# Layer 1 in another order: batch 0 is split around batch 1, and the weights are converted over 19 steps

## The chip, the cores and the metric

One core of a Trainium2 chip. The metric is the device time of one execution in microseconds (us), the median of several runs. TensorE is PE in the rows, VectorE DVE, ScalarE ACT, GpSimd POOL, SyncE SP.

## What is computed

Three stages in a row, over 4 batches of 512 tokens and 32 states, with 8 heads of 64:

```
scores = x @ state.T / 8        a  = softmax(scores)      xread = a  @ state
scores2 = state @ x.T / 8       a2 = softmax(scores2)     sread = a2 @ x
x1 = concat(xread, sread)                        # 2176 rows of 512
h  = x1 @ w_in  (512 x 2048);   g = h - tanh(h);          x2  = g @ w_out
h2 = x2 @ w_in2 (512 x 2048);   g2 = h2*tanh(softplus(h2)); out = g2 @ w_out2
```

The weights arrive as 64-bit floats, everything else as 32-bit floats.

## The kernel before

**Layer 1** runs in steps. A step is one column tile (128 of the 2048 inner columns) of one batch (512 tokens), so a batch has 16 steps, 0 to 15, and the state rows of all batches have 4 more. The list `seq` sets the order: batch 0, batch 1, batch 2, the states, batch 3.

In each step `up_x` makes the tile's 128x512 of h with six matmuls into one of two PSUM banks (h0, h1 in turn). It doesn't form x1: it multiplies the transposed softmax weights of the batch (`ath`, `atl`, a large and a small part) by the product of the states and w_in (`swp` when it is made, `swh` and `swl` when it is split), which `sw(b, c)` makes for four column tiles at a time. `elem1` then takes tanh on ScalarE (`t<-h`), subtracts on VectorE (`t<-h,t`), which frees the bank, and splits the result into `gh` (ScalarE) and `gl` (VectorE). Five steps later `down_x` multiplies this by w_out: 4 x 3 matmuls into four PSUM banks a0 to a3 (`acc`), which collect all 16 tiles of a batch and are then copied out to SBUF (`y`, or a half of a tile named `wide`), two by ScalarE and two by VectorE. For the first three tiles of batch 0 (`PLAIN`) nothing is split, and `down_x` issues 4 full-precision matmuls `acc<-t,w` in place of the 12.

**Weights.** A 128x512 piece of 64-bit weights is loaded by `load_next` into one of three `st` and three `wide` buffers; the queue `pending` sets the order of the loads. `conv_steps` makes it 32-bit: two ScalarE instructions (`w<-st` and `r<-st`, or `<-wide`), then one on VectorE (`w<-w,r`). Pieces i0 to i15 are of w_in, four for each group of four column tiles; pieces o0 to o15 are of w_out, one for each column tile, and are split too (`wh`, `wl`). Batch 0 uses each piece first; all the pieces then stay in SBUF for the later batches.

**Attention** of a batch is side work, hung on step numbers by `at(step, ...)`: transposes of x (`xtp`), scores (`sct`), their transposes (`sc`), maximum, subtraction, exp and norm (`mx`, `a`, `sm`), then `at_a`, which transposes the weights `a` (`atp`) and splits them into `ath`, `atl`. The other softmax goes through `at_exp_t`, `at_read_t` (`e2p`), `at_sread` (`srd`) and `at_sturn` (`srt`). Work on the second layer's weights (`bg`) runs beside layer 1, paced by the list `pace`; it stores its results through POOL's queue.

**Order.** Each engine works through its own queue in order. The first part of every queue, up to the bar in `FIRST_STEPS`, is pinned by hand; the rest is put in order by a scheduler when the kernel is built, by the order in which the code is written and by what has to be ready.

Layer 2 begins after layer 1's last step and takes nearly half of the time. The change does not touch its code.

Of the kernel before, what the change touches and what calls it, by code (L numbers as in the profile page):

```python
# [23 lines left out]
PLAIN = 3  # L24
# [2 lines left out]
MOST = 3  # L27
ROOM = 20
BACK = 2

# [8 lines left out]
FIRST_STEPS = """  # L39
    k4 s0 x0 X0 x1 X1 x2 X2 x3 X3 w0 w0 c0 C0 C1 k2 w0 t0 m0 t1 w1 w1 f0 b0 p0 P0 m1 e0 p1 P1 b1  # L40
    p2 e1 P2 u0 p3 P3 v0 y0 k6 w2 u1 v1 w2 h0 z2 q1 y1 h1 g0 l0 w1 l1 Q0 Q1 | f1 g1 w2 f2 g2
    w3 w3 w3 z2 f3 g3 w4 w4 w4
"""


class Unit:
# [29 lines left out]
def attention_moe_kernel(  # L76
# [296 lines left out]
    def conv_w1i(c, k):  # L373
        W1I[c, k] = conv32(("w1i", c, k))
# [6 lines left out]
    def conv_w1o(t):  # L381
        if t < PLAIN:
            W1O[(t,)] = conv32(("w1o", t))
        else:
            conv_split(W1O, ("w1o", t), t)

    def split_w1o(t):
        w = W1O[(t,)]
        W1O[(t,)] = split(w.t, name="w")
        put(w)  # L390

    def rows(w, t):
        return w[t * 128:(t + 1) * 128, :]
# [111 lines left out]
    def at_exp(b, j):  # L505
        sc_t(b, j)
        sc_max(b, j)
        sc_sub(b, j)
        sc_exp(b, j)
# [127 lines left out]
    def sw(b, c):  # L637
        if c:
            rhs = [[W1I[c, k].t for k in range(KD)]]
        else:  # L640
            rhs = [[w1i_tile(0, k, f) for k in range(KD)] for f in range(4)]
        ps = by_head("swp", b, rhs)
        for j in range(2):
            SW[b, c, j] = split(ps[j], name="sw")
        if b == B - 1:
            for k in range(KD):
                put(W1I.pop((c, k)))
            if not W1I:
                put(SB)
# [58 lines left out]
        return AC.activation(out=dst, in_=src, func=ACTF.Copy)  # L708

    def down_x(b, t):  # L710
        if t == 0:
            ACC[b] = [acc_bank(i) for i in range(KD)]
        if b == 0 and t < PLAIN:
            g = [G.pop((b, t))]
            w = W1O[(t,)]
        else:
            g = G.pop((b, t))
            wh, wl = W1O[(t,)]
        for i in range(KD) if b != 2 else (KD - 1, *range(KD - 1)):
            s = slice(i * 128, (i + 1) * 128)  # L720
            if len(g) == 1:
                TE.matmul(
                    out=ACC[b][i], lhsT=w.t[:, s], rhs=g[0].t, start=t == 0, stop=t == NT - 1
                )
            else:
                mm3p(
                    ACC[b][i], wh.t[:, s], wl.t[:, s], g[0].t, g[1].t, t == 0, t == NT - 1
                )
            if t == NT - 1:
                y = get("y")  # L730
                evac(y.t, ACC[b][i], i)
                Y[b, i] = y
        put(*g)
        if b == B - 1:
            put(*W1O.pop((t,)))
# [314 lines left out]
    wi = [  # L1050
        (("w1i", c, k), cols(w1i, c, k) if c else ftile(w1i, k)) for c in range(4) for k in range(KD)
    ]
    pending.extend(wi[:5])
    for t in range(NT):
        pending.append((("w1o", t), rows(w1o, t)))
        pending.extend(wi[5 + t:6 + t])
    for c in range(4):
        for k in range(KH):
            for j in (k, k + KH):
# [31 lines left out]
    seq = []  # L1091
    start = {}
    for b in (0, 1, 2, "s", 3):
        start[b] = len(seq)
        seq += [("x", b, t) for t in range(NT)] if b != "s" else [("s", c) for c in range(4)]
    start["2"] = len(seq)

    for s in range(16):
        at(s, lambda s=s: conv_w1o(s))
        if s < 11:  # L1100
            at(s, lambda s=s: conv_w1i((s + 5) // 4, (s + 5) % 4))
        if s in (2, 6, 11):
            at(s, lambda s=s: sw(0, s // 4 + 1))
        if s < PLAIN:
            at(start[1] + max(0, s - 1), lambda s=s: split_w1o(s))
    for b in (1, 2, 3):
        for c in range(4):
            at(start[b] + 4 * c - 2, lambda b=b, c=c: sw(b, c))
    for j in range(2):
        at(12 + j, lambda j=j: at_exp(1, j))  # L1110
        at(13 + j, lambda j=j: at_norm(1, j))
        for b in range(2):
            k = start[1] + 4 + 2 * b + 4 * j
            at(k, lambda b=b, j=j: at_exp_t(b, j), 1)
            at(k + 3 - b, lambda b=b, j=j: at_read_t(b, j), 1)
            if j:
                at(k + 4 - b, lambda b=b: at_sread(b), 1)
                at(k + 6 - b, lambda b=b: at_sturn(b), 1)
    when = {2: (3, 4, 5, 7, 8, 9, 10, 11, 12, 13, 15, 16), 3: (1, 3, 4, 5, 7, 8, 9, 11, 12, 12, 13, 15)}
    for b in (2, 3):  # L1120
        at(start[b - 1] - (b - 2), lambda b=b: load_x(b))
        for i, f in zip(when[b], at_steps(b), strict=True):
            at(start[b - 1] + i, f)
    for b in (1, 2, 3):
        at(start[b] - (3 if b > 1 else 1), lambda b=b: at_a(b))
    at(start[3], lambda: bg.extend(pieces_y(0) + list(late)))
    pace = [(start[1] + 8, 0), (start["s"], 52), (start["2"], 96)]
    done = [0]

    def keep_pace(i):  # L1130
# [101 lines left out]
        for t in tiles:  # L1232
            put(*(Unit(t[:, h * 512:(h + 1) * 512], None) for h in range(2)))

    at(start[1], widen)

    def up(q):
        if q[0] == "x":
# [89 lines left out]
```

## Time and profile before

| | us |
|---|---|
| median of 3 runs (714.16 to 715.76) | 715.24 |
| the profiled execution | 715.61 |
| its span, first to last instruction | 713.8 |
| TensorE busy in the span | 703.0 (98%) |
| VectorE busy | 467.0 (65%) |
| ScalarE busy | 350.7 (49%) |

The profiled execution is 1.8 us longer than its span, and 0.37 us longer than the median. Shares of busy time are means over very different stages. [...]

### The profile page before, as it was taken

The numbers are of one execution on the slowest core, as the hardware profiler recorded it, in microseconds if no ns is written. First come the engines' busy times: TensorE is split into PE (matmuls) and PEld (weight loads), VectorE is DVE, ScalarE is ACT, GpSimd is POOL, SyncE is SP. The second block draws the span as 40 slices with busy tenths as digits, with TensorE's granted clock in tenths as the row PEclk, the third lists the DMA queues.
The fourth block names the chain that finished last, engine by engine and source line by source line (L and its number), as shares of the span: only waits on it lengthen the run. The fifth ranks groups of instructions, "written<-read, shape, count | busy, mean of one in ns | idle before, by whom it ended". The sixth has DMA issues, their size and how long they took to land.

```text
span 713.8 us, 10569 instructions
## 1 busy us (share of the span) xinstructions
PE 703.0 (98%) x3978; PEld 562.3 (79%) x3978; DVE 467.0 (65%) x797; ACT 350.7 (49%) x631; POOL 70.5 (10%) x110
## 2 busy tenths in 40 slices
PE   8899999999999999999999999999999999999998
PEld 6467877777777898777878888888888888888886
DVE  5899855676659757898657875547753455545654
ACT  5999545555566656867546342234333223222320
POOL 0000010005202234410304100000000000000000
PEclk9999999999999999999999999999999999999999
DMA  9885110005536458692958654444966244322003
GB/s 289 318 309 189 61 59 2 31 30 171 217 109 213 163 184 274 203 356 91 344 213 299 225 174 153 145 141 134 313 208 199 93 159 157 124 77 85 1 1 132
DMA packets 52643, 118.66 MB, mean 166 GB/s; under 512 B 7280, under 2 KB 11632, under 8 KB 52592
## 3 DMA queue, kind: packets, MB, share of 16 engines
q1 hardware_dynamic: 44272, 90.72, 38.1%
q0 software_dynamic: 8320, 27.27, 10.5%
q8 instruction: 31, 0.51, 0.3%
q14 instruction: 20, 0.16, 0.1%
HBM read 88.34 MB, written 29.62 MB: 165 GB/s over the span
## 4 chain that ended last, share of the span: by engine, by line
PE 87%; ACT 5%; issue 2%; DMA 2%; DVE 2%; POOL 1%; SPq 1%; POOLq 0%; ACTq 0%
PE acc L63 48%; PE h L63 32%; PE swp L63 2%; PE hs L63 2%; ACT r L63 1%; ACT w L63 1%; DMA x<-in_x_dram 1%; DMA wide<-in_x_dram 1%; PE xtp L63 1%; POOL wi L261 1%; ACT t L63 1%; DVE wide L63 1%; ACT gh L63 1%; PE sct L63 1%; PE e2p L63 0%
## 5 line engine op out<-in xcount | busy, mean ns | idle before, releaser
L63 PE MATMUL acc<-wo,gh 128*128 128x512 f32 (+1 forms) x548 | 168.1, 388 | 0.0
L63 PE MATMUL h<-yh,ws 128*128 128x512 f32 x448 | 156.8, 391 | 0.1
L63 PEld LDWEIGHTS acc<-wo,gh 128*128 128x128 f32 x548 | 102.1, 188 | 20.9 <-ACT gh L63 0.4
L63 DVE TENSOR_TENSOR wide<-acc,wide 128x512 f32<-128x512 f32 (+1 forms) x92 | 62.9, 684 | 74.6 <-PE acc L63 73.3
L63 PE MATMUL acc<-wo,gl 128*128 128x512 f32 (+1 forms) x274 | 106.3, 388 | 0.0
L63 PE MATMUL acc<-gh,wh 128*128 128x512 f32 x244 | 99.4, 408 | 0.0
L63 PEld LDWEIGHTS h<-yh,ws 128*128 128x128 f32 x448 | 84.1, 188 | 17.8 <-DVE mt L63 0.5
L63 PE MATMUL acc<-gh,wl 128*128 128x512 f32 x244 | 95.7, 392 | 0.0
L63 PE MATMUL acc<-gl,wh 128*128 128x512 f32 x244 | 95.2, 390 | 0.0
L63 PE MATMUL h<-yl,ws 128*128 128x512 f32 x224 | 87.3, 390 | 0.0
L63 DVE TENSOR_TENSOR wide<-h,wide 128x512 f32<-128x512 f32 x94 | 64.6, 687 | 27.9 <-ACT wide L63 13.9
L63 DVE TENSOR_TENSOR gl<-wide,gh 128x512 fp32r<-128x512 f32 x72 | 49.7, 690 | 47.4 <-ACT gh L63 47.3
L63 ACT ACTIVATE wide<-wide 128x512 f32<-128x512 f32 x47 | 29.7, 632 | 85.3 <-DVE wide L63 85.3
L63 ACT ACTIVATE wide<-h 128x512 f32<-128x512 f32 x41 | 24.4, 596 | 81.0 <-PE h L63 80.1
L63 PEld LDWEIGHTS acc<-wo,gl 128*128 128x128 f32 x274 | 51.4, 188 | 11.0 <-DVE gl L63 0.4
L63 PEld LDWEIGHTS acc<-gh,wh 128*128 128x128 f32 x244 | 45.9, 188 | 17.5 <-issue 5.6
L63 PEld LDWEIGHTS acc<-gh,wl 128*128 128x128 f32 x244 | 45.8, 188 | 11.4 <-issue 1.2
L63 PE MATMUL h<-ath,swh 128*128 128x512 f32 x128 | 51.5, 403 | 1.8 <-DVE t L63 1.0
L63 PEld LDWEIGHTS acc<-gl,wh 128*128 128x128 f32 x244 | 46.0, 188 | 8.4
L63 PE MATMUL h<-ath,swl 128*128 128x512 f32 x128 | 50.4, 394 | 0.0
L63 PE MATMUL h<-atl,swh 128*128 128x512 f32 x128 | 50.0, 390 | 0.0
L63 ACT ACTIVATE gh<-wide 128x512 fp32r<-128x512 f32 x72 | 45.5, 631 | 7.3 <-DVE wide L63 5.5
(168 smaller groups left out, 1019.9 us busy)
## 6 DMA issues: line engine op xcount, KB each, us to landing
ws<-wi SPq DMA_DIRECT2D x128, 256.0 KB, 3.9
wo<-wo SPq DMA_DIRECT2D x64, 256.0 KB, 3.9
st<-in_moe_w_in_dram SPq DMA_DIRECT2D x27, 512.0 KB, 5.7
st<-in_moe_w_out_dram SPq DMA_DIRECT2D x22, 512.0 KB, 4.9
wi<-wh POOLq DMA_DIRECT2D x32, 256.0 KB, 3.8
wi<-wl POOLq DMA_DIRECT2D x32, 256.0 KB, 4.4
wide<-in_moe_w_out_dram SPq DMA_DIRECT2D x10, 512.0 KB, 5.3
wo<-wh POOLq DMA_DIRECT2D x16, 256.0 KB, 5.6
```

Of the source, the lines that this page charges most:

```text
L63: i = fn(*args, **kw)
L261: nc.gpsimd.dma_start(out=d, in_=v if len(d.shape) == 2 else v.rearrange("p (g e) -> p g e", g=2))
```

## The change

`seq` now takes the first four tiles of batch 0, all 16 of batch 1, the other 12 of batch 0, then batch 2, the states and batch 3 as before. The sums of batch 0's first four tiles leave the four PSUM banks after tile 3 (two copies on ScalarE and two on VectorE) and wait in SBUF; when the other 12 tiles are done, four VectorE additions put the two parts together, where four copies stood before. So the four banks are handed over at one place more than before: after batch 0's tile 3, after batch 1, after batch 0's tile 15, after batch 2.

Layer 1 starts with pieces i0 to i3; i4 is no longer converted ahead of the first step. The list `CONVERTED` gives the pieces of each of 19 steps, and the loads come in that order; before, the steps 0 to 15 took one piece of w_out each and the first eleven a piece of w_in too. What batch 1 needs for its first step (exp and norm of both halves, `at_a`) moves from steps 12 to 15 to steps 0 to 3. The products of the states and w_in come two steps ahead of use as before, by batch and group. The other softmax of batches 0 and 1 moves from steps 20 to 31 to steps 12 to 21, that of batch 2 stays, and for batch 3 the first transposes of x go from steps 33 and 35 to step 35. The background work starts at step 22 in place of 24.

```diff
-    w3 w3 w3 z2 f3 g3 w4 w4 w4
+    w3 w3 w3 z2 f3 g3
...
+CONVERTED = (
+    "o0", "o1 i4", "o2", "o3 i5", "i6", "o4 i7", "i8 o5", "i9 o6", "i10 i11", "o7 i12", "o8 i13",
+    "o9 i14", "o10 i15", "o11", "o12", "o13", "o14", "o15",
+)
...
     def down_x(b, t):
-        if t == 0:
+        starts = t in ((0, PART) if b == 0 else (0,))
+        stops = t in ((PART - 1, NT - 1) if b == 0 else (NT - 1,))
+        if starts:
             ACC[b] = [acc_bank(i) for i in range(KD)]
...
-            if t == NT - 1:
+            if stops and (b, i) in Y:
+                V.tensor_tensor(out=Y[b, i].t, in0=ACC[b][i], in1=Y[b, i].t, op=ALU.add)
+            elif stops:
                 y = get("y")
                 evac(y.t, ACC[b][i], i)
...
-    for b in (0, 1, 2, "s", 3):
-        start[b] = len(seq)
-        seq += [("x", b, t) for t in range(NT)] if b != "s" else [("s", c) for c in range(4)]
+    for b, ts in (
+        (0, range(PART)), (1, range(NT)), (0, range(PART, NT)), (2, range(NT)), ("s", range(4)),
+        (3, range(NT)),
+    ):
+        start.setdefault(b, len(seq))
+        seq += [("x", b, t) if b != "s" else (b, t) for t in ts]
...
-    for s in range(16):
-        at(s, lambda s=s: conv_w1o(s))
-        if s < 11:
-            at(s, lambda s=s: conv_w1i((s + 5) // 4, (s + 5) % 4))
-        if s in (2, 6, 11):
-            at(s, lambda s=s: sw(0, s // 4 + 1))
-        if s < PLAIN:
-            at(start[1] + max(0, s - 1), lambda s=s: split_w1o(s))
...
+    for t in range(PLAIN):
+        at(PART + t, lambda t=t: split_w1o(t))
...
-        at(12 + j, lambda j=j: at_exp(1, j))
-        at(13 + j, lambda j=j: at_norm(1, j))
...
+        at(j, lambda j=j: at_exp(1, j))
+        at(1 + j, lambda j=j: at_norm(1, j))
+    for b, times in ((0, (12, 13, 13, 15, 16, 17)), (1, (15, 16, 16, 17, 20, 21))):
...
-    when = {2: (3, 4, 5, 7, 8, 9, 10, 11, 12, 13, 15, 16), 3: (1, 3, 4, 5, 7, 8, 9, 11, 12, 12, 13, 15)}
+    when = {2: (3, 4, 5, 7, 8, 9, 10, 11, 12, 13, 15, 16), 3: (3, 3, 4, 5, 7, 8, 9, 11, 12, 12, 13, 15)}
...
-    pace = [(start[1] + 8, 0), (start["s"], 52), (start["2"], 96)]
+    pace = [(start[2] - 10, 0), (start["s"], 52), (start["2"], 96)]
```

**What this moves on the engines.** First place: TensorE between its fourth tile of h (batch 0, tile 3) and its fifth. Before, the full-precision sums stand among the tiles, and the product for batch 0's tiles 4 to 7 (`swp`, eight wide matmuls) comes ahead of tile 4:

```order
L63 MATMUL acc_554<-t,w 128x512
L63 MATMUL acc_555<-t,w 128x512
L63 MATMUL acc_552<-t,w 128x512
L63 MATMUL swp<-w,sbt 32x512 x8
L63 MATMUL acc_553<-t,w 128x512
L63 MATMUL h<-ath,swh 128x512
L63 MATMUL h<-atl,swh 128x512
L63 MATMUL acc_554<-t,w 128x512
```

Now the fifth tile is batch 1's first. The product for batch 1 (32 narrow matmuls) and both transposes of batch 1's softmax weights stand ahead of it:

```order
L70 MATMUL acc_605<-t,w 128x512
L70 MATMUL acc_606<-t,w 128x512
L70 MATMUL acc_607<-t,w 128x512
L70 MATMUL acc_608<-t,w 128x512
L70 MATMUL swp<-w,sbt 32x128 x32
L70 MATMUL acc_605<-t,w 128x512
L70 MATMUL acc_606<-t,w 128x512
L70 MATMUL acc_607<-t,w 128x512
L70 MATMUL atp<-ident,a 128x128 x4
L70 MATMUL acc_608<-t,w 128x512
L70 MATMUL atp<-ident,a 128x128 x4
L70 MATMUL h<-ath,swh 128x512 x2
```

Eight of the twelve full-precision matmuls have moved behind tile 3, and two transposes of `a`, which stood behind tile 15, now stand ahead of tile 4. The second transpose has one such matmul between it and the first.

Second place: VectorE around its seventh and eighth subtraction `t<-h,t`. Before, between these two:

```order
L63 TENSOR_TENSOR t<-h,t 128x512
L63 SCALAR_TENSOR_TENSOR w<-w,r 128x512
L63 CAST wh<-w 128x512
L63 TENSOR_TENSOR gl<-t,gh 128x512
L63 TENSOR_TENSOR swl<-swp,swh 128x512 x2
L63 TENSOR_TENSOR wl<-w,wh 128x512
L63 SCALAR_TENSOR_TENSOR w<-w,r 128x512 x3
L63 TENSOR_TENSOR t<-h,t 128x512
```

Now, between the same two:

```order
L70 TENSOR_TENSOR t<-h,t 128x512
L70 CAST wh<-w 128x512
L70 TENSOR_TENSOR wl<-w,wh 128x512
L70 TENSOR_TENSOR gl<-t,gh 128x512
L70 TENSOR_TENSOR wl<-w,wh 128x512
L70 TENSOR_TENSOR swl<-swp,swh 128x512 x2
L70 COPY y<-acc_606 128x512
L70 COPY y<-acc_608 128x512
L70 TENSOR_TENSOR t<-h,t 128x512
```

The copies of the second and fourth bank are new; they stand behind a `gl` and two `swl`, which wait for ScalarE's `gh` and `swh`. ScalarE's copies of the first and third bank stand right behind that `gh`, with one `r<-st` between them.

Third place: TensorE at the first turn of a state read (`srt`, batch 0's). Such side products share two PSUM banks with `swp`, in turn. Before, the turn stands in the middle of a step's sums, shortly behind the products for batch 2, whose banks VectorE's `swl` frees:

```order
L63 MATMUL swp<-w,sbt 32x128 x32
L63 MATMUL acc_1307<-gh,wh 128x512
L63 MATMUL acc_1307<-gl,wh 128x512
L63 MATMUL acc_1307<-gh,wl 128x512
L63 MATMUL acc_1308<-gh,wh 128x512
L63 MATMUL acc_1308<-gl,wh 128x512
L63 MATMUL acc_1308<-gh,wl 128x512
L63 MATMUL acc_1309<-gh,wh 128x512
L63 MATMUL acc_1309<-gl,wh 128x512
L63 MATMUL acc_1309<-gh,wl 128x512
L63 MATMUL srt<-ident,wide 128x128
L63 MATMUL acc_1310<-gh,wh 128x512
```

Now batch 0's turn comes in step 17, behind a whole tile of h:

```order
L70 MATMUL h<-atl,swh 128x512
L70 MATMUL h<-ath,swl 128x512
L70 MATMUL h<-ath,swh 128x512
L70 MATMUL h<-atl,swh 128x512
L70 MATMUL h<-ath,swl 128x512
L70 MATMUL srt<-ident,sr 128x128
L70 MATMUL e2p<-ident,scs 128x128 x4
L70 MATMUL acc_797<-gh,wh 128x512
```

The nearest products of a group stand three tiles of h ahead of it; before, nine sums lay between.

## Rows read from the trace of the kernel before

**Rows 1.** The page: busy time, and TensorE in 40 slices of the span.

```profile
PE 703.0 (98%) x3978; PEld 562.3 (79%) x3978; DVE 467.0 (65%) x797; ACT 350.7 (49%) x631; POOL 70.5 (10%) x110
...
PE   8899999999999999999999999999999999999998
```

**Rows 2.** Waits of TensorE: waited for, us in total, times, longest.

```profile
PE h L63 <- DVE t L63: 1.0, 1, 1.0
...
PE xtp L63 <- DMA wide<-in_x_dram: 0.9, 1, 0.9
PE h L63 <- ACT swh L63: 0.7, 1, 0.7
PE srt L63 <- DVE swl L63: 0.6, 1, 0.6
PE swp L63 <- DVE w L63: 0.6, 2, 0.3
```

**Rows 3.** Windows: length, busy PE, PEld, DVE, ACT, POOL, then clock, DMA share, GB/s.

```profile
20.00:40.00 20.00, 17.93 (x126) 9.48 (x125) 17.24 (x34) 20.00 (x44) 0.00 (x0) 1.00 0.86 313
40.00:60.00 20.00, 19.74 (x90) 13.86 (x89) 18.57 (x32) 19.95 (x38) 0.00 (x0) 1.00 0.85 301
160.00:180.00 20.00, 19.26 (x207) 14.79 (x207) 12.74 (x25) 12.24 (x23) 10.14 (x14) 1.00 0.52 175
180.00:200.00 20.00, 19.12 (x102) 14.65 (x100) 11.56 (x20) 11.07 (x20) 4.92 (x7) 1.00 0.48 181
```

**Rows 4.** Timeline of TensorE: start, us, what, [idle before, releaser].

```profile
23.79 0.45 PE L63 MATMUL swp<-w,sbt 64*32 64x128 f32 x16
25.28 0.47 PE L63 MATMUL h<-ath,swh 128*128 128x512 f32 x1 [1.03 <-DVE t L63]
...
41.58 3.60 PE L63 MATMUL acc<-t,w 128*128 128x512 f32 x8
44.61 0.79 PE L63 MATMUL h<-ath,swh 128*128 128x512 f32 x1
...
54.58 0.39 PE L63 MATMUL acc<-gh,wl 128*128 128x512 f32 x1
54.80 0.39 PE L63 MATMUL h<-ath,swh 128*128 128x512 f32 x1
...
73.75 0.60 PE L63 MATMUL sc<-ident,scs 128*128 128x128 f32 x4
74.11 0.48 PE L63 MATMUL acc<-gh,wh 128*128 128x512 f32 x1
...
82.95 1.16 PE L63 MATMUL swp<-w,sbt 64*32 64x128 f32 x64
```

**Rows 5.** Timeline of ScalarE, same columns.

```profile
21.38 0.71 ACT L63 ACTIVATE r<-wide 128x512 uint32<-128x512 uint32 x1
...
23.05 0.63 ACT L63 ACTIVATE t<-h 128x512 f32<-128x512 f32 x1
...
28.00 0.74 ACT L63 ACTIVATE w<-st 128x512 f32<-128x512 f32 x1
28.55 0.74 ACT L63 ACTIVATE r<-st 128x512 uint32<-128x512 uint32 x1
29.11 0.67 ACT L63 ACTIVATE t<-h 128x512 f32<-128x512 f32 x1
29.59 0.75 ACT L63 ACTIVATE w<-wide 128x512 f32<-128x512 f32 x1
```

**Rows 6.** Timeline of VectorE: two instructions back to back, and two copies of banks.

```profile
48.13 0.68 DVE L63 TENSOR_TENSOR t<-h,t 128x512 f32<-128x512 f32 x1
48.73 0.68 DVE L63 SCALAR_TENSOR_TENSOR w<-w,r 128x512 uint32<-128x512 uint32 x1
...
105.12 1.28 DVE L63 COPY wide<-acc 128x512 f32<-128x512 f32 x2
```

**Rows 7.** Chain that ended last, the load of batch 3's x.

```profile
176.39 6.49 DMA wide<-in_x_dram
```

More of the change, by code (lines that the diff above doesn't have):

```diff
@@ L29 @@
 BACK = 2
+PART = 4
 FIRST_LOADS = "s0123wwt4567wwww"
@@ L722, in down_x @@
                 TE.matmul(
-                    out=ACC[b][i], lhsT=w.t[:, s], rhs=g[0].t, start=t == 0, stop=t == NT - 1
+                    out=ACC[b][i], lhsT=w.t[:, s], rhs=g[0].t, start=starts, stop=stops
                 )
@@ L726, in down_x @@
                 mm3p(
-                    ACC[b][i], wh.t[:, s], wl.t[:, s], g[0].t, g[1].t, t == 0, t == NT - 1
+                    ACC[b][i], wh.t[:, s], wl.t[:, s], g[0].t, g[1].t, starts, stops
                 )
-            if t == NT - 1:
+            if stops and (b, i) in Y:
+                V.tensor_tensor(out=Y[b, i].t, in0=ACC[b][i], in1=Y[b, i].t, op=ALU.add)
+            elif stops:
                 y = get("y")
@@ L1052, in attention_moe_kernel @@
     ]
[L1053 to L1056, printed above, removed]
+    pending.extend(wi[:KD])
+    for key in " ".join(CONVERTED).split():
+        n = int(key[1:])
+        pending.append((("w1o", n), rows(w1o, n)) if key[0] == "o" else wi[n])
     for c in range(4):
@@ L1106, in attention_moe_kernel @@
-    for b in (1, 2, 3):
-        for c in range(4):
-            at(start[b] + 4 * c - 2, lambda b=b, c=c: sw(b, c))
-    for j in range(2):
-        at(12 + j, lambda j=j: at_exp(1, j))
-        at(13 + j, lambda j=j: at_norm(1, j))
[L1112 to L1118, printed above, removed]
@@ L1119, in attention_moe_kernel @@
-    when = {2: (3, 4, 5, 7, 8, 9, 10, 11, 12, 13, 15, 16), 3: (1, 3, 4, 5, 7, 8, 9, 11, 12, 12, 13, 15)}
+    for b, ts in (
[4 more added lines that the diff above has]
+        seq += [("x", b, t) if b != "s" else (b, t) for t in ts]
+    start["2"] = len(seq)
+    for s, keys in enumerate(CONVERTED):
+        for key in keys.split():
+            n = int(key[1:])
+            if key[0] == "o":
+                at(s, lambda n=n: conv_w1o(n))
+            else:
+                at(s, lambda n=n: conv_w1i(n // KD, n % KD))
@@ new lines, in attention_moe_kernel @@
+    for t in range(PLAIN):
+        at(PART + t, lambda t=t: split_w1o(t))
+    for b in range(B):
+        for c in range(not b, 4):
+            k = seq.index(("x", b, 4 * c)) - 2
+            at(k, lambda b=b, c=c: sw(b, c))
+    for j in range(2):
+        at(j, lambda j=j: at_exp(1, j))
+        at(1 + j, lambda j=j: at_norm(1, j))
+    for b, times in ((0, (12, 13, 13, 15, 16, 17)), (1, (15, 16, 16, 17, 20, 21))):
+        for k, f in zip(
+            times,
+            (
+                lambda b=b: at_exp_t(b, 0), lambda b=b: at_read_t(b, 0),
+                lambda b=b: at_exp_t(b, 1), lambda b=b: at_read_t(b, 1),
+                lambda b=b: at_sread(b), lambda b=b: at_sturn(b),
+            ),
+            strict=True,
+        ):
+            at(k, f, 1)
@@ L1120, in attention_moe_kernel @@
+    when = {2: (3, 4, 5, 7, 8, 9, 10, 11, 12, 13, 15, 16), 3: (3, 3, 4, 5, 7, 8, 9, 11, 12, 12, 13, 15)}
     for b in (2, 3):
-        at(start[b - 1] - (b - 2), lambda b=b: load_x(b))
+        at(16 * (b - 1) - 2 * b + 5, lambda b=b: load_x(b))
         for i, f in zip(when[b], at_steps(b), strict=True):
-            at(start[b - 1] + i, f)
+            at(16 * (b - 1) + i, f)
     for b in (1, 2, 3):
@@ L1233, in widen @@
             put(*(Unit(t[:, h * 512:(h + 1) * 512], None) for h in range(2)))
-    at(start[1], widen)
+    at(len(CONVERTED), widen)
     def up(q):
```

## Prediction

> **What bounds the kernel now.** The page first: TensorE is busy for 703.0 of 713.8 us, and in the 40 slices it falls below 9 tenths only in the first two and the last [rows 1]. So there are 10.8 us of idle TensorE at most, and a change that issues the same matmuls, as this one does, can win only a part of them. The view of TensorE's waits says where they lie [rows 2]: leaving out the start (first loads, first transposes), a tile of h waits 1.0 us for a subtraction on VectorE and another 0.7 us for `swh`, the products of the groups 0.6 us for converted weights, a turn of the state read (`srt`) 0.6 us and a transpose of batch 3's x 0.9 us for its load. The windows put the first three into 20 to 60 us, where ScalarE is busy 20.00 and 19.95 of 20 us, and the last two into 160 to 200 us, where TensorE lacks 0.74 and 0.88 us [rows 3]. [...]
>
> ScalarE's 40 full microseconds are conversions. One half of a conversion follows the other after 0.55 to 0.56 us, and a tanh takes 0.48 us until the next begins [rows 5]. VectorE starts one per 0.60 us [rows 6]. The clock of this stretch is thus ScalarE's queue, and TensorE waits where it needs something that stands deep in it. That makes the sum below a matter of queue positions: what stands ahead of the thing waited for.
>
> **The change part by part.**
>
> *The first tile's subtraction.* Two halves of i4 no longer stand ahead of the first tanh: ScalarE goes from the `r` at 21.38 straight to it, at 21.9 in place of 23.05 [rows 5]. The subtraction then ends near 23.7, before the small products end at 24.24 (23.79 and 0.45), and the third tile starts there and not at 25.28: the 1.03 us wait goes [rows 4]. The 0.7 and 0.6 us in rows 2 hang on batch 0's tile 4 and on early pieces of w_in; tile 4 is no longer the fifth tile, so these go as well. That is 2.3 us off.
>
> *What comes in their place.* Batch 1's first tile is the fifth one now. Its transposes (`atp`) take the two banks of the products right before them, so they wait for VectorE's two `swl`; the second waits for the last norm multiplication too, which stands behind these two, a reciprocal and a `gl`. Those wait for ScalarE's `swh` and `gh`. Ahead of that `gh`, from the `r` at 21.38 on, the changed kernel's order gives ScalarE 16 conversion halves, 4 tanh, 5 full instructions of other kinds (taken as 0.52, between the two) and 4 small ones (no row shows one alone; taken as 0.33): 9.0 + 1.9 + 2.6 + 1.3 = 14.8, so `gh` starts at 36.2. VectorE gets through `swl`, reciprocal, `gl` and the multiplication at about 38.2. TensorE arrives earlier. From 24.24 it has two tiles of h (six matmuls of 0.22 each, 1.35), both `sc` (0.36 and a slow start behind it, 0.4 each: 73.75 to 74.11), eight full-precision matmuls, the products (1.1: 82.95 and 1.16 less the overlap) and one `atp`, taken as an `sc` of the same shape. Four full-precision ones take 3.03 us and stretch the next by 0.40 (41.58 to 44.61, 0.79 in place of 0.39), so 0.86 each [rows 4]. That is 24.24 + 2.7 + 0.8 + 6.9 + 1.1 + 0.4 = 36.1: a new wait of about 2 us.
>
> *The hand-over after batch 0's tile 3.* Batch 1's first sums need the banks. Up to the `gh` of the seventh tile ScalarE has 30 halves, 7 tanh, 15 others and 6 small ones from 21.38 on: 16.8 + 3.4 + 7.8 + 2.0 = 30.0, so it starts at 51.4 and ends at 52.0 (0.6 us). Behind it VectorE has `gl`, `wl`, two `swl` (four at 0.60) and then the copy of the second bank; two copies of a bank took 1.28, so 0.64 [rows 6]: free at 55.0. Then three banks' sums, nine matmuls, 2.0: the fifth tile's sums, which follow the eighth tile of h, end at 57.0. Before, the sums at this place ended at 54.80 [rows 4]. The new order has two `sc` and two `atp` more in front of this point, 1.7 to 1.8 us that are saved later, so 56.6 would be even. TensorE itself would be at the second bank at 54.80 - 2.0 + 1.8 - 2.3 + 2.0 = 54.3, earlier than 55.0, so the copy ends last. **The early stretch gives nothing: 0.4 us worse**, with ScalarE's queue setting the time as before. The bounds: 2.3 us better (no new wait) and 1.5 us worse, if VectorE idles ahead of the copy as it did in 40 to 60 us, 1.4 of 20 us [rows 3], so 1.1 us in the 15 us between the two places.
>
> Past this point ScalarE has less to do per step than before and catches up; loads are not late either, since each piece is converted later than the piece of the same number in the queue of loads was before, and ScalarE did not idle for one in 20 to 60 us [rows 3].
>
> *The late waits.* Batch 3's x is loaded in step 31 still, and its first transpose comes two steps later, about 9 us; the load took 6.49 us from issue [rows 7], and the wait was 0.9. It goes. The turn that waited 0.6 for `swl` no longer follows the products that hold its bank: three tiles of h lie between. It goes too. By the windows both are worth **1.6 us** [rows 3]. The bounds are 1.6 and 0 (other reads and turns, moved to steps 12 to 21, wait as long).
>
> *The other hand-overs.* After batch 0's tile 15 VectorE makes four additions from PSUM. The trace has none of this form from this stage in the rows; a copy of a bank took 0.64, so 2.6 for four if they begin when the last sum ends. A tile of h and two transposes of x cover 2.2. Between 0 and 0.4, taken as 0.1, since the first three banks are done ahead of the last. Before, the same four banks changed hands after batch 0, with copies at 105.12 [rows 6], and the waits show nothing for it [rows 2]. [...]
>
> **Sum.** +0.4 - 1.6 + 0.1 = -1.1 us on the profiled span of 713.8. The profiled execution (715.61, 1.8 us around the span) is 0.37 above the median, so I put the difference to the median: 715.24 - 1.1 = **714.1 us**. A difference of 0.2%, 1.43 us, is about what a measurement of this kernel can tell from no change; this one is smaller.
>
> **The rivals.**
>
> *No new wait at the hand-over.* If VectorE gets through its queue sooner than the 0.60 steps say, ScalarE's own copies are last: the first starts at 51.9, the second behind one `r` at 53.0, free at 53.6, and two banks' sums end at 55.0, 1.6 better than 56.6. With the late waits gone: 715.24 - 1.6 - 1.6 = 712.0. For it: TensorE's distance to the copy is only 0.7 us. Against it: VectorE was busy 18.57 of 20 us there [rows 3]. 0.18.
>
> *The late waits stay, elsewhere.* The reads of batches 0 and 1 now stand in steps 12 to 21, behind conversions that run until step 18. 715.24 + 0.4 + 0.1 = 715.7. 0.18.
>
> *Slower: background work.* It starts two steps earlier, while batch 0 still has ten tiles and batch 2's attention is under way. Before, the 40 us in which POOL first stores its results are the ones in which TensorE waits 1.62 us [rows 3], 0.04 per us: a turn or transpose waits for what a conversion delays on VectorE or in POOL's queue. At this rate over the 80 us of steps 14 to 31 it is 3.2 in place of 1.6, so 715.24 + 0.5 + 1.6 = 717.3. It decides from 2.5 us of waits in that stretch on. Against it: VectorE is busy for 12 of 20 us there. 0.12.
>
> *The hand-overs are not covered.* TensorE stands for all four additions, 2.6 in place of 0.1: 716.6. The hand-over of before speaks against it [rows 2, 6]. 0.05. [...]
>
> **How the numbers follow.** My forecast has 0.47, and about half of it, with the early stretch 0.3 better than worked out, is over the 1.43 us. Faster: 0.18 + 0.24 = 0.42. Same: 0.23 + 0.18 + 0.02 = 0.43. Slower: 0.12 + 0.03 = 0.15. The range goes from below the first rival, 711.6 (the early bound would give 711.4), to 716.5, which leaves out most of the third and half of the fourth; the forecast's own is 713.0 to 715.4.
>
> **What would show it.** The third tile of h starts at 24.2 with no wait on VectorE; a wait of about 2 us on VectorE's `a` at the second `atp`, at 36 to 38 us; a wait of 0.5 to 1.5 us at the second bank of the first batch 1 sums, on the copy of `y`, and their end near 57; ScalarE full from 20 to 55 us and with gaps from 62 us on; no TensorE wait for batch 3's x, none at a `srt`. The forecast fails if the two early waits are missing (then ScalarE is not the clock that I take it for), or if the windows of 100 to 200 us lack more than 1.6 us of TensorE.

## The result and the profile after

The changed kernel takes 719.16 us (median of 4 runs, 718.32 to 720.61), the kernel before 714.91 on the same chip (714.16 to 715.76). The ratio is 1.0058, with a 95% interval of 1.0042 to 1.0073: 0.6% slower, clear of no change, and outside the range that was predicted. The profiled execution of the changed kernel took 719.03 us with a span of 717.3, against 713.8 before.

The page (busy time; then PE, its load of weights left out, and the granted clock in 40 slices) answers to [rows 1]:

```profile
PE 704.4 (98%) x3978; PEld 564.2 (79%) x3978; DVE 467.8 (65%) x801; ACT 351.4 (49%) x631; POOL 70.5 (10%) x110
...
PE   8999999999899998999999999999999999999998
```

Idle TensorE has grown from 10.8 to 12.9 us, and PE's own busy time from 703.0 to 704.4. The matmuls are the same, and the granted clock of the whole was 0.997 (1.000 in the kernel before), so a part of this is a slower clock, whose place is found below. The slices fall below 9 tenths in the first, the eleventh (179 to 197 us), the fourteenth (233 to 251), the sixteenth (269 to 287) and the last; the three in the middle are new, and in the fourteenth the timeline shows no idle time. TensorE's waits (us in total, times, longest), against [rows 2]:

```profile
PE acc L70 <- DVE y L70: 2.4, 2, 1.4
PE acc L70 <- DVE wide L70: 2.1, 1, 2.1
PE warm L70 <- DVE warm L1200: 1.5, 1, 1.5
PE sc L70 <- DVE swl L70: 1.3, 1, 1.3
PE atp L70 <- DVE swl L70: 0.6, 1, 0.6
PE xtp L70 <- DVE swl L70: 0.6, 1, 0.6
PE atp L70 <- ACT r L70: 0.5, 1, 0.5
```

All five waits of before are gone, and six other lines have come (the seventh, `warm`, is at the start of both kernels). The windows say where (columns as in [rows 3]):

```profile
20.00:40.00 20.00, 18.93 (x157) 10.75 (x157) 18.79 (x40) 20.00 (x43) 0.00 (x0) 1.00 0.88 287
40.00:60.00 20.00, 18.96 (x102) 13.44 (x101) 18.86 (x33) 19.52 (x38) 0.00 (x0) 1.00 0.76 253
...
100.00:180.00 80.00, 79.93 (x607) 62.16 (x606) 49.61 (x93) 43.13 (x78) 15.72 (x22) 1.00 0.31 99
180.00:200.00 20.00, 18.05 (x95) 13.62 (x95) 13.42 (x22) 12.87 (x23) 4.36 (x8) 1.00 0.70 234
200.00:240.00 40.00, 38.72 (x228) 29.38 (x227) 30.26 (x63) 24.22 (x46) 9.49 (x14) 1.00 0.40 132
240.00:280.00 40.00, 37.93 (x354) 33.45 (x353) 26.99 (x48) 26.30 (x47) 14.42 (x22) 1.00 0.73 251
280.00:320.00 40.00, 40.00 (x194) 31.05 (x193) 33.49 (x54) 26.25 (x48) 7.99 (x13) 0.96 0.41 145
```

Up to 180 us the changed kernel is no worse than the old one; 100 to 180 us is full. What it loses lies in three places from 180 us on, and behind the third the clock is down (0.96 in the last window, with no idle time). TensorE's timeline there, and at the early places that the prediction named:

```profile
18.12 0.47 PE L70 MATMUL h<-ath,swh 128*128 128x512 f32 x1
...
23.10 0.50 PE L70 MATMUL h<-ath,swh 128*128 128x512 f32 x1
...
34.89 0.66 PE L70 MATMUL atp<-ident,a 128*128 128x128 f32 x4 [0.59 <-DVE swl L70]
...
36.88 0.63 PE L70 MATMUL atp<-ident,a 128*128 128x128 f32 x4 [0.47 <-ACT r L70]
...
53.50 0.50 PE L70 MATMUL acc<-gh,wh 128*128 128x512 f32 x1 [1.04 <-DVE y L70]
...
55.68 0.39 PE L70 MATMUL h<-ath,swh 128*128 128x512 f32 x1
...
188.82 0.66 PE L70 MATMUL xtp<-ident,wide 128*128 128x128 f32 x4 [0.56 <-DVE swl L70]
...
191.30 0.47 PE L70 MATMUL acc<-gh,wh 128*128 128x512 f32 x1 [1.39 <-DVE y L70]
...
230.70 0.66 PE L70 MATMUL sc<-ident,wide 128*128 128x128 f32 x4 [1.28 <-DVE swl L70]
...
279.51 0.56 PE L70 MATMUL acc<-wh,gh 128*128 128x512 f32 x1 [2.07 <-DVE wide L70]
279.87 0.63 PE L70 MATMUL acc<-wl,gh 128*128 128x512 f32 x1
280.30 0.63 PE L70 MATMUL acc<-wh,gl 128*128 128x512 f32 x1
```

At 191.30 the additions after batch 0's tile 15 look guilty. VectorE's timeline shows that they begin late:

```profile
186.70 0.68 DVE L70 TENSOR_TENSOR swl<-swp,swh 128x512 fp32r<-128x512 f32 x1
187.48 0.69 DVE L70 TENSOR_TENSOR gl<-wide,gh 128x512 fp32r<-128x512 f32 x1
188.09 0.68 DVE L70 TENSOR_TENSOR swl<-swp,swh 128x512 fp32r<-128x512 f32 x1
188.69 2.47 DVE L70 TENSOR_TENSOR y<-acc,y 128x512 f32<-128x512 f32 x4
```

The products (`swp`) were done at 183.9, the sums of tile 15 at 186.9. `swl` waits for `swh`, and `swh` stands in ScalarE's order behind a conversion. ScalarE's timeline, at this place and at the states' hand-over:

```profile
176.20 0.63 ACT L70 ACTIVATE gh<-wide 128x512 fp32r<-128x512 f32 x1 [0.20 <-DVE wide L70]
180.81 0.66 ACT L70 ACTIVATE r<-st 128x512 uint32<-128x512 uint32 x1 [3.98 <-DMA wi<-wl]
181.37 0.66 ACT L70 ACTIVATE wide<-st 128x512 f32<-128x512 f32 x1
182.83 0.63 ACT L70 ACTIVATE wh<-wide 128x512 fp32r<-128x512 f32 x1 [0.80 <-DVE wide L70]
183.37 0.58 ACT L70 ACTIVATE wide<-h 128x512 f32<-128x512 f32 x1
...
185.84 0.59 ACT L70 ACTIVATE swh<-swp 128x512 fp32r<-128x512 f32 x1
...
187.35 0.58 ACT L70 ACTIVATE swh<-swp 128x512 fp32r<-128x512 f32 x1
...
225.50 0.63 ACT L70 ACTIVATE wh<-w 128x512 fp32r<-128x512 f32 x1 [2.70 <-DMA wi<-wl]
...
274.55 0.68 ACT L70 ACTIVATE w<-st 128x512 f32<-128x512 f32 x1 [2.12 <-DMA st<-in_moe_w_out_dram]
...
276.75 1.05 ACT L70 ACTIVATE swh<-swp 128x512 fp32r<-128x512 f32 x2
```

This is the reading that matters. For 3.98 us ScalarE stands, that is, does nothing: the next instruction in its order is the `r` of a background piece, and the slot (a 128x512 buffer in SBUF) that it writes to is still being stored by POOL (`wi<-wl`). The tanh of the tile of h that TensorE had finished at 178.9 waits behind it until 183.37, then the two `swh`, VectorE's `swl`, the additions, the banks. Nothing overtook the `r` in these 3.98 us. Nor does anything elsewhere: in the trace of the changed kernel all 801 of VectorE's instructions begin in the order of the program, and ScalarE's do too.

At 225.50 the same happens for another store (2.70 us), ahead of the wait at 230.70; at 274.55 for a load that hasn't landed (2.12 us), ahead of `gh`, `swh`, `swl` and the copies of batch 2's banks.

The length of a stand alone doesn't say what it costs. The kernel before has one of 3.25 us, and the changed kernel with the start at step 24 (experiment 4) one of 4.27, and TensorE has no wait in the ten microseconds behind either:

```profile
246.39 0.66 ACT L63 ACTIVATE w<-st 128x512 f32<-128x512 f32 x1 [3.25 <-DMA wi<-wl]
```

```profile
262.36 0.66 ACT L70 ACTIVATE w<-st 128x512 f32<-128x512 f32 x1 [4.27 <-DMA st<-in_moe_w_in_dram]
```

The three that the changed kernel pays for end 3 to 8 us ahead of TensorE's wait, with the `swh` of new products and, at two of them, banks that change hands in between.

### The profile page after: what moved, and what is told of

The parts are those of the page before. It is cut to its first block, busy times and chain, and to the rows that moved or that the text cites. A ratio compares the mean times of both kernels' runs of the same rounds, so it can differ in the third digit from the quotient of the medians.

```text
span 717.3 us, 10593 instructions
## 1 busy us (share of the span) xinstructions
PE 704.4 (98%) x3978; PEld 564.2 (79%) x3978; DVE 467.8 (65%) x801; ACT 351.4 (49%) x631; POOL 70.5 (10%) x110
## 4 chain that ended last, share of the span: by engine, by line
PE 70%; issue 15%; ACT 6%; POOL 5%; DVE 3%; DMA 1%; POOLq 0%; ACTq 0%; DVEq 0%
PE acc L70 39%; PE h L70 26%; POOL wi L268 3%; PE hs L70 2%; ACT w L70 1%; ACT r L70 1%; POOL wo L268 1%; PE swp L70 1%; DMA wi<-wh 1%; ACT wh L70 1%; ACT gh L70 1%; PE xtp L70 1%; ACT t L70 0%; DVE wl L70 0%; ACT swh L70 0%
## 5 line engine op out<-in xcount | busy, mean ns | idle before, releaser
L70 DVE TENSOR_TENSOR wide<-acc,wide 128x512 f32<-128x512 f32 (+1 forms) x78 | 53.3, 683 | 61.8 <-PE acc L70 60.5
L70 DVE TENSOR_TENSOR wide<-h,wide 128x512 f32<-128x512 f32 x103 | 70.8, 687 | 27.9 <-ACT wide L70 15.8
L70 DVE TENSOR_TENSOR gl<-wide,gh 128x512 fp32r<-128x512 f32 x81 | 55.9, 691 | 48.2 <-ACT gh L70 47.9
L70 ACT ACTIVATE wide<-h 128x512 f32<-128x512 f32 x51 | 30.3, 594 | 83.8 <-PE h L70 82.4
L70 ACT ACTIVATE gh<-wide 128x512 fp32r<-128x512 f32 x81 | 51.2, 632 | 13.7 <-DVE wide L70 11.9
```

What stands on the lines that cost most here:

```text
L70: i = fn(*args, **kw)
```

## The experiments

Theory A: the background pieces, two steps earlier, make ScalarE stand for stores and loads, and TensorE's new waits come from there. Theory B: the hand-over with its four additions costs by itself. All are edits of the changed kernel. Nothing of the computation is left out in any run.

**1. Pieces held to the counts of the kernel before** (`ran_before` is the list of them by step).

```
-                goal = n0 + (n1 - n0) * (i + 1 - s0) / (s1 - s0)
+                goal = ran_before[i]
```

> The changed kernel with one thing put back: the number of background pieces that have run after each step follows the list of the kernel before (1 piece by step 24, 8 by step 31, 40 by step 48), not the changed kernel's own pace (6, 13 and 46). Theory A, background work: pieces that run earlier make ScalarE stand for a store (4.0 us ahead of 180.8) and for a load (2.1 us ahead of 274.6), and TensorE's waits of 2.0 us at 188 to 191, 1.3 at 230 and 2.1 at 278 us with the slower clock behind it (1.6) come from there. Then these waits go and the time is 719.2 - 5 to 7 = 712 to 714.5 us. Theory B, the hand-over: the four additions on VectorE after batch 0's tile 15 are the price wherever the pieces stand. Then the wait of 1.4 us at the first sums behind it stays, and those at 230 and 278 us, which follow other work, stay as well: 718 to 720 us.

713.73 us, ratio 0.9992 (0.9978 to 1.0006). The waits at 188 to 191 and at 278 are gone, with the additions in place; one of 1.29 us at 229 stays. Theory A. The list was only a ceiling: for want of free slots 7 pieces had run by step 32, where the kernel before had run 11.

**2. Copies at the hand-over, additions later.**

```
-                V.tensor_tensor(out=Y[b, i].t, in0=ACC[b][i], in1=Y[b, i].t, op=ALU.add)
+                z = get("z")
+                evac(z.t, ACC[b][i], i)
+                at(37 + i, lambda i=i, z=z: add_y(b, i, z))
```

> The changed kernel with its background pace kept, but the four banks of batch 0's second part are copied out as batch 0's were in the kernel before (two copies on ScalarE, two on VectorE, into four more slots), and the four additions follow in SBUF three to six steps later. Theory A (background work): VectorE is late for another reason, ScalarE's stand ahead of it, so of the 2.0 us at 188 to 191 at least 1 stays, and the other waits as well: 717.5 to 719.5 us. Theory B (the hand-over): the wait of 1.4 us on VectorE's y goes: 717.5 us or less, with no stand at this place. The slots taken may move pieces by a few steps; the windows around 180 to 200 us are what is read.

718.56 us, 1.0051 (1.0036 to 1.0066). TensorE still waits at the same place, 2.69 us for `swl` and 0.79 for a copy, behind a stand of ScalarE of 3.40 us for a store. Theory B falls. (`add_y`, not shown, adds the copy to the first part in SBUF.) The waits at 230 and 278 are gone, which theory A did not foresee: up to step 35 the pieces run as in the changed kernel, but from step 36 on the four slots taken put them up to eight pieces behind it.

**3. Both.**

> Both edits at once: background pieces held to the counts of the kernel before, and the four additions later in SBUF behind copies. If the two losses are of different origin they add up and this is the fastest of the four: 711.5 to 713.5 us. Theory A alone gives the same as the pieces alone within 0.7 us; theory B alone the same as the copies alone.

722.42 us, 1.0121 (1.0086 to 1.0156): a miss by 9 us. Between steps 36 and 52 the four slots more push the pieces back two to six behind experiment 1, and ScalarE stands for loads, 3.80 us ahead of 276.5 the longest; TensorE waits 2.1 us at 250, 2.88 at 280 and 1.22 at 324. So neither the additions nor the mean lead of the pieces decides, but what stands where.

**4. Only the start of the pace, 24 in place of 22.**

```
-    pace = [(start[2] - 10, 0), (start["s"], 52), (start["2"], 96)]
+    pace = [(start[2] - 8, 0), (start["s"], 52), (start["2"], 96)]
```

> The changed kernel with only the start of the background pace put back, from step 22 to step 24; the rest of the pace and the additions stay. Theory A with the start as its cause (my rival of the prediction: two steps earlier): most of the loss at 180 to 240 us goes, 714 to 717 us. If the cause is not the start but which slot a piece takes and which store or load is still under way at that moment, the pieces catch up within some steps and new stands appear at other places: 716 to 720 us. Theory B: 719 us, as the changed kernel.

713.61 us, 0.9983 (0.9973 to 0.9992): 5.5 us come back from one number. VectorE and TensorE at the hand-over of batch 0, additions unchanged:

```profile
186.86 0.68 DVE L70 TENSOR_TENSOR swl<-swp,swh 128x512 fp32r<-128x512 f32 x1
187.46 2.47 DVE L70 TENSOR_TENSOR y<-acc,y 128x512 f32<-128x512 f32 x4
```

```profile
189.09 1.03 PE L70 MATMUL xtp<-ident,wide 128*128 128x128 f32 x8
190.08 0.47 PE L70 MATMUL acc<-gh,wh 128*128 128x512 f32 x1
```

The same four additions, 2.47 us, now begin 1.2 us earlier (2.3 us, counted from the first tile of h, which starts at 19.20 in this profile and at 18.12 in the other), and the sums behind them start with no wait.

**5 and 6. Start at 23, and at 26.** The same line with 9 and with 6.

> The changed kernel with the background pace started at step 23, one step later than it does and one earlier than the kernel that ran at 713.6 us. By the program's own list of free slots the pieces then stand as in the changed kernel from step 27 on (10 run by step 28, 16 by 32, 46 by 48, where a start at 24 gives 5, 11 and 40). Theory A (the pieces' places after step 27 decide, through ScalarE's stands for stores and loads): 717.5 to 720 us, with ScalarE standing 3 to 4 us for a store ahead of 181 us. Rival A2 (each step of an earlier start costs by itself, some 2.8 us per step by the two known points): 716 to 717 us.

> The same start moved the other way, to step 26. From step 31 on the pieces stand as with a start at 24. Theory A: 713 to 715 us, the same as with 24. Rival A2 (each step costs by itself): 709 us or less, since another 2.8 us per step would come off.

718.53 us (1.0059, 1.0038 to 1.0079) and 713.91 (0.9992, 0.9982 to 1.0002). It is a step between 23 and 24, not a slope: theory A, and not a price per step. With 23 ScalarE stands 3.27 us for a store ahead of 182.5 and TensorE waits in the same three places.

**7. Slots given back nine pieces after their store was issued, not six.**

```
-HOLD = 6
+HOLD = 9
```

> The changed kernel, start at step 22 kept, but a slot whose content has been sent off by POOL comes back into use nine pieces later in place of six, so that ScalarE and VectorE take slots whose stores are longer under way. This holds pieces back too (15 in place of 22 by step 36, 40 in place of 46 by step 48), since fewer slots are free. Theory A: ScalarE's stands for stores (4.0 us ahead of 180.8, 2.7 ahead of 225.5) go or fall under 1 us each, and TensorE's waits of 2.0 and 1.3 us behind them with them: 712.5 to 716 us. If the stands have to do with the start and not with slots that are taken too soon: 718 to 720 us.

720.01 us, 1.0070 (1.0046 to 1.0095): the time is a miss, the mechanism is not. Between 95 and 255 us ScalarE has no stand of half a microsecond or more for a store, and TensorE no wait of 0.2 us at 188 to 191 or at 230. But loads come late behind it:

```profile
262.76 0.66 ACT L70 ACTIVATE r<-st 128x512 uint32<-128x512 uint32 x1 [4.79 <-DMA st<-in_moe_w_in_dram]
272.54 0.68 ACT L70 ACTIVATE w<-st 128x512 f32<-128x512 f32 x1 [3.25 <-DMA st<-in_moe_w_in_dram]
...
289.01 0.66 ACT L70 ACTIVATE r<-st 128x512 uint32<-128x512 uint32 x1 [2.12 <-DMA st<-in_moe_w_out_dram]
```

TensorE waits 2.66 us at 278, 0.82 at 298 and 1.85 at 321. So the first two waits of the changed kernel come from slots taken while their store is under way; the third is of another kind, a load. The edit also holds pieces back (13 in place of 16 by step 32), so this run alone does not part the slot from the place; the releaser in the timeline (`wi<-wl`) does.

**8. Batch 3's x loaded one step later.**

```
-        at(16 * (b - 1) - 2 * b + 5, lambda b=b: load_x(b))
+        at(16 * (b - 1) - b + 3 if b == 3 else 17, lambda b=b: load_x(b))
```

> The changed kernel with batch 3's x loaded one step later (step 32 in place of 31), so that POOL's queue puts its four issues of x, 2.9 us, behind the stores of the pieces and not ahead of them; all else as it is, the count of pieces per step too. ScalarE's stand of 4.0 us ahead of 180.8 is for the store issued last, at 176.8. If the x issues in front of the stores are what makes this store late, it lands some 2.9 us sooner, the stand falls to about 1 us and the wait of 2.0 us at 188 to 191 goes, while those at 230 and 278 us stay: 716.5 to 718 us. If the queue isn't the cause (too many pieces at once are): 718.5 to 720 us.

717.22 us, 1.0034 (1.0021 to 1.0048): the number was right, the reason not. The x issues still stand among the stores, the last `wi<-wl` is issued at 176.84 as before, and ScalarE's stand is 4.09 us. TensorE's wait behind it is 0.52 in place of 1.95 and the one at 230 is gone; ScalarE's order is another there, with a stand of 1.89 us ahead of 220.04 in place of 2.70 ahead of 225.50. Whether POOL's queue makes the store late was not decided.

**9 to 12. At most three pieces a step around the states, with the start at 22 and at 24; the copies of batch 0's first four tiles split by halves; both.**

```
-                for _ in range(MOST + (start["s"] - 2 <= i < start[3] or i >= start[3] + 6)):
+                for _ in range(MOST + (i >= start[3] + 6)):
...
-                evac(y.t, ACC[b][i], i)
+                evac(y.t, ACC[b][i], i // 2 if b == 0 else i)
```

> The changed kernel with at most three background pieces a step around the states (steps 46 to 51), where it may run four; 50 in place of 58 have run by step 51. Between 255 and 280 us the changed kernel moves 7.92 MB with its DMA queues at 92% of the 16 engines, the kernel before 5.70 MB at 67%, and there ScalarE stands 2.1 us for a load ahead of 274.6, TensorE 2.1 us behind it and at the lower clock for 7 us (1.6 us). If the crowd of pieces at this place is the cause, the stand falls under 1 us and 2 to 3.7 us come off; the waits at 188 to 230 us stay: 715.5 to 717.5 us. If the loads are late because they are issued one behind the other in any case, the wait moves to another step and the time stays at 718 to 720 us.

> The start at step 24 and at most three pieces a step around the states. With the start at 24 one wait of 1.1 us is left at this place (274.5 us) and one of 0.4 at 295. If the crowd is the cause, these go: 712 to 713.3 us. If a load is late wherever the pieces stand: 713.5 to 717 us, as in the runs that held pieces back in other ways.

> The start at step 24, and the four banks of batch 0's first four tiles are copied out by ScalarE (first and second bank) and VectorE (third and fourth) in place of in turn. The wait of 1.2 us at the second bank of batch 1's first sums, which hangs on VectorE's copy behind its queue of four, goes; VectorE's first copy is then needed two banks later, 1.4 us. If nothing else ends there: 1.2 us off, 712.2 to 712.8 us. If ScalarE's queue is the clock of this stretch whoever copies, its second copy, moved ahead of one conversion half, puts the next tiles off as much: 713.3 to 714 us.

> The start at 24 with both: three pieces a step around the states and the copies split by halves. If both edits do what they are for, they add up: 711 to 712.3 us, the fastest of all. If the waits only move: the worse of the two single runs, within 0.7 us.

Start 22 with three a step: 722.31 us, 1.0107 (1.0085 to 1.0130), outside both expectations. Its ScalarE at the states' hand-over:

```profile
277.47 0.66 ACT L70 ACTIVATE w<-st 128x512 f32<-128x512 f32 x1 [6.46 <-DMA wi<-wl]
278.04 0.61 ACT L70 ACTIVATE wh<-s 128x512 fp32r<-128x512 f32 x1
278.56 0.61 ACT L70 ACTIVATE gh<-wide 128x512 fp32r<-128x512 f32 x1
279.08 1.07 ACT L70 ACTIVATE swh<-swp 128x512 fp32r<-128x512 f32 x2
```

TensorE waits 5.02 us behind it, though the DMA engines moved less between 255 and 280 us than in the changed kernel (272 against 317 GB/s). That doesn't clear the crowd of transfers: between 255 and 275 us the DMA engines moved nearly as much as there (308 against 323 GB/s), and the lower mean comes mostly from the last 5 us (126 against 291), where ScalarE already stands. Up to experiment 12 the runs with a wait of 2 us or more at this place moved 287 to 333 GB/s between 255 and 275 us, those with a wait under 0.2 moved 224 to 288. So a crowd may help to make a load or store late; it was neither shown nor ruled out. Start 24 with three: 714.05 us (0.9987, 0.9977 to 0.9997), where the wait at 274 goes and one of 1.54 us at 316 comes. Start 24 with the split copies: **713.19 us, 0.9976 (0.9965 to 0.9987), the fastest by its median**, within the intervals of 4 and 12; the wait at the second bank, 1.0 us with the start at 24, falls to 0.4. Both edits: 713.57 us (0.9979, 0.9970 to 0.9989), so they don't add up.

**13 and 14. No piece in step 49; none in steps 48 and 49.**

```
     def keep_pace(i):
+        if i in (49,):
+            return
```

> The changed kernel, but no background piece is run in step 49, whose conversions stand in ScalarE's order ahead of the copies at the states' hand-over; they follow from step 50 on. In the program's order one `r` and one full conversion half less far stand between batch 2's last products and those copies, where the changed kernel has six halves. If a conversion that isn't ready ahead of the copies is what TensorE waits for at 277 us (2.1 us and 1.6 us of slower clock), this wait goes and the one at 188 to 191 stays: 715 to 717 us. If the pieces' number or the DMA load decides, whatever stands ahead of the copies: 718.5 to 722 us.

> The same with no piece in steps 48 and 49. The pieces that ran in step 47 and before now stand ahead of the copies. If what counts is whether a conversion ahead of the copies is ready, the outcome hangs on these: between 715 and 720 us, and TensorE's wait at the states' hand-over follows ScalarE's stand for a load or store ahead of its `gh` and `swh`, long where that is long, none where it is under 1 us.

715.94 us (1.0025, 1.0008 to 1.0042) and 714.78 (1.0004, 0.9995 to 1.0014). At the states' hand-over the wait of 2.07 us falls under 0.2 in both, and the clock stays at 1.00 between 270 and 300 us (0.94 in the changed kernel). In the second run ScalarE reaches `swh` and the copies without a stand for a load or store:

```profile
270.39 0.63 ACT L70 ACTIVATE gh<-wide 128x512 fp32r<-128x512 f32 x1 [0.76 <-DVE wide L70]
270.93 1.07 ACT L70 ACTIVATE swh<-swp 128x512 fp32r<-128x512 f32 x2
271.88 0.60 ACT L70 ACTIVATE wide<-acc 128x512 f32<-128x512 f32 x1
```

The other two waits stay (0.89 to 1.84 us at the hand-over of batch 0, 1.0 to 1.1 at 230). The third wait, too, is a conversion in ScalarE's order ahead of the copies. (Both runs also thin the transfers between 240 and 280 us, to 217 and 194 GB/s, in the changed kernel 251, so they do not decide about the crowd.)

**15. Early start, but no piece in steps 32 to 34.** The same two lines with (32, 33, 34).

> The changed kernel with its early start at step 22 kept and 13 pieces run by step 31, but no piece in steps 32 to 34, the three of which stood ahead of batch 0's hand-over; from step 35 on the pieces stand as with a start at 24. If the places of the pieces from step 32 on decide, and not the start: 713 to 714.5 us, with no wait at 188 to 191, none at 230 and about 1.1 at 274. If the early start costs by itself: 716 us or more.

714.42 us, 0.9994 (0.9984 to 1.0003). At the hand-over of batch 0 0.34 us are left of 1.95, nothing at 230, and 0.71 at 276. The early start does little harm by itself (0.8 us more than the start at 24, with intervals that overlap); the three pieces of step 32 and those that follow it do.

All runs in one table. "Pieces" are those that have run by step 32, by the program's own count; the waits are TensorE's, in us, from the timelines (a dash is under 0.2).

```
kernel                      pieces  median   at 188-191  at 230  states' hand-over
changed                       16    719.16      1.95      1.28      2.07
 1 pieces as before            7    713.73       -        1.29       -
 2 copies, additions later    16    718.56      3.48       -         -    (1.27 at 300)
 3 both                        7    722.42       -         -        2.88  (2.1 at 250, 1.22 at 324)
 4 start 24                   11    713.61       -         -        1.06
 5 start 23                   16    718.53      1.93      1.06      2.98
 6 start 26                   11    713.91       -         -        0.71
 7 slots back after nine      13    720.01       -         -        2.66  (0.82 at 298, 1.85 at 321)
 8 x one step later           16    717.22      0.52       -        2.46
 9 three a step               16    722.31      1.24      0.69      5.02
10 start 24, three a step     11    714.05       -         -         -    (1.54 at 316)
11 start 24, copies split     11    713.19       -         -        0.28
12 start 24, both             11    713.57       -         -         -    (1.54 at 315)
13 none in 49                 16    715.94      1.84      1.14       -
14 none in 48 and 49          16    714.78      0.89      1.01       -
15 none in 32 to 34           13    714.42      0.34       -        0.71
```

## Why the prediction was wrong

One step failed, and with it left out the sum agrees in part by luck. The other steps are taken first, with times counted from the first tile of h, since that begins 1.08 us earlier in the profile of the changed kernel (18.12 against 19.20), which need not be the change's: with the same first steps it begins anywhere between 18.12 and 19.85 us (last section).

*The first tile's subtraction.* Right. The third tile of h starts at 23.10 without a wait, 4.98 us after the first; predicted were 24.2, 5.0 after it. The 1.03, 0.7 and 0.6 us of [rows 2] are gone.

*What comes in their place.* Right in place, half in size: 0.59 us at the first `atp` and 0.47 at the second, 1.1 in place of 2. No row shows the 0.33 us that the sum takes for a small instruction of ScalarE, and this profile has less: the four up to the `gh` (`swh` of 128x128) take 0.37 us for the first two and 0.32 for the others, 0.7 in place of 1.3, and the `gh` begins 14.1 us behind the `r` (34.43 against 20.29), where 14.8 were added up. The page names ScalarE's `r` at the second one, but VectorE's multiplication of `a` ended at 36.73 and the transposes begin at 36.88: the name is that of the signal that came last by the profile, and the times fit the wait that was worked out.

*The hand-over after batch 0's tile 3.* Right. The wait at the second bank is 1.04 us on `y`, the sums end at 55.68, 37.56 after the first h; 37.4 would be even, 37.8 was predicted. So 0.2 us worse in place of 0.4, by the prediction's estimate of 1.8 us for the transposes that moved ahead of this point; TensorE's idle time up to it fell from 2.37 to 2.15 us. ScalarE is busy for 34.95 of the 35 us from 20 to 55, as foreseen; its first gap, 0.43 us, stands ahead of 58.78, not behind 62.

*The late waits.* Right: no wait for batch 3's x, none at a `srt`, and 160 to 180 us is full.

*The other hand-overs.* Right, though the profile of the changed kernel seems to say otherwise. The 1.39 us at 191.30 aren't the additions' price: with the start at 24 the same additions cost nothing (experiment 4), and taken off the path they leave the wait (experiment 2). At this place one more hand-over of the same four banks has a price in these two runs only where VectorE is late: 1.39 us with the start at 22, none with 24.

*The sum.* The number is right without the early start of the background work; its parts are not, so this is luck in part. With the pace start put back and all else changed, the time is 713.61 against 714.84, 1.2 us off; 1.1 were predicted. From the first h to the end that run's profile is 1.0 us shorter than before (693.6 against 694.6). But up to the first matmul of the states it is 3.1 us shorter (230.76 against 233.87, from the first h), where the sum had all of its 1.1, and from there to layer 2's first h it is 2.1 us longer (93.65 against 91.55), where the sum had nothing. Of the 3.1 us, 1.9 are idle time of TensorE (2.16 in place of 4.06) and the rest shorter busy time for as many matmuls, which was not followed up. Of the 2.1 us, 1.06 and 0.29 are the waits at 276 and 296 behind ScalarE, so the background work still costs in this run.

*The step that failed* is the start of the background work two steps earlier, which the prediction put among the rivals ("Slower: background work", 0.12 and 1.6 us) and left out of the sum, a term put at nothing. The reason that it gave against it, "VectorE is busy for 12 of 20 us there", was the wrong measure: VectorE and ScalarE had time (busy for 11.1 to 12.7 of each 20 us from 160 to 200 us in the kernel before [rows 3]), what counted was the order. A piece's conversion that wasn't ready held up everything behind it on ScalarE, for 3.98, 2.70 and 2.12 us; the rival had looked for the wait on VectorE and in POOL's queue. It cost 5.5 us (719.16 less 713.61) and not 1.6: in the profile 1.95 and 1.28 us of waits for stores, 2.07 for a load, and some 1.6 us more because the eight matmuls behind it follow each other in 0.43 us, not 0.23. These come to 6.9. With the start at 24, 1.35 us of waits are left (1.06 and 0.29), so the sum of the difference is 5.5, where the profiles show 5.6 from the first h to the end (699.2 against 693.6). The 1.6 us of slower clock had no place in the prediction's sum; in the windows that it was drawn from the granted clock is 1.00 [rows 3]. The place was off as well: 100 to 200 us lack 2.0, over the 1.6 at which the forecast was to fail, but under the 2.5 that were to decide for this rival; the rest follows up to 300 us.

Why two steps did so much could be seen before the run in the program's order. A piece starts only when ten slots are free. The old order had fewer from step 21 to 27, so its pieces were held back whatever the start said (1 had run by step 27, and by the program's own count a start at 22 would have moved none of them). In the new order slots are free at step 22, and 7 pieces run by then.

What stays open: why a given store or load is late, and whether the crowd of transfers has a part in it. Experiments 3, 7 and 9 show that fewer pieces, or pieces later, can cost as much as the early ones. The pairing of a piece with a slot or a load shifts with every edit, and nothing here foretells where it falls.

## What to carry to other kernels

When background work shares an engine's queue with work on the path, ask not only whether the engine has time but whether each background instruction is ready when its turn comes (here ScalarE stood for 3.98 us ahead of one `r`, with a tanh ready behind it from 178.9 us on): look for the idle time of that engine put down to a DMA, and follow what stands behind it; here a stand cost only where TensorE needed that soon (1.95 us of waits behind one of 3.98, none behind one of 4.27). A change that frees buffers earlier can start such work earlier (here 7 pieces by step 27 in place of 1), so a start step that changed nothing before can begin to bite; put it back first when a reordering loses time (here 5.5 us). A wait named after the last instruction before it (here the additions) is tested by taking that instruction off the path and by making it early, which here gave the same answer from two sides.

## What the runs showed of the hardware

*The clock after a wait.* In five runs several matmuls behind TensorE's wait in the states' hand-over began 0.43 us apart, where those after them, of the same shape, began 0.23 apart (in the changed kernel the granted clock was 0.50 from 280 to 283 us, 3.4 us in all and not the 7 of one expectation), and the granted clock between 270 and 300 us was 0.94 in the changed kernel (2.07 us of wait), 0.94 in experiments 3, 5 and 8 (2.88, 2.98, 2.46) and 0.89 in experiment 9 (5.02). It stayed at 1.00 in experiment 7, with 2.66 us of wait at the same place. So the length of the wait alone doesn't say whether the clock falls.

*Stores.* The page's list of DMA issues (KB each, median us from issue to landing) has for the changed kernel:

```profile
wi<-wh POOLq DMA_DIRECT2D x32, 256.0 KB, 4.5
wi<-wl POOLq DMA_DIRECT2D x32, 256.0 KB, 4.9
```

In the page of the kernel before, the same two have 3.8 and 4.4 us.

*The start.* The sixteen changed orders share their first steps, yet the first tile of h starts between 18.12 and 19.85 us, as TensorE waits for the loads of x for less than 0.2 us in all or for up to 1.9. This is not all of it: in experiment 13 the tile starts at 19.20 with no such wait listed. One profile's first 20 us can thus hide or feign a microsecond, so distances are counted here from a point behind the loads.
